# First layer in seven products for 15 blocks in place of 10, with sums kept in PSUM banks, in a chunked-attention and two-layer kernel

## The chip, the cores and the metric

The kernel runs on one core of a Trainium2 chip. The metric is the device time of one execution in microseconds (us). The core's engines work side by side, each through its own list of instructions in order: PE (TensorE, the matrix products), DVE (VectorE), ACT (ScalarE), POOL (GpSimd), and SP, which here only issues DMAs. PE reads from SBUF and writes into PSUM, which has eight banks of 512 f32 per partition. POOL also issues the DMAs that load and convert f32 to f16.

## What is computed

```python
# q, k, v: (8, 8, 576, 64) f32; batch, heads, sequence, head size
q_c, k_c, v_c = (a.reshape(B, H, 9, 64, D) for a in (q, k, v))     # chunks of 64
scores = np.matmul(q_c, k_c.transpose(0, 1, 2, 4, 3)) / np.sqrt(D)
scores = scores - scores.max(-1, keepdims=True)
attn = np.exp(scores); attn = attn / (attn.sum(-1, keepdims=True) + 1e-09)
x = np.matmul(attn, v_c) ... .reshape(4608, 512)                   # tokens x (heads * D)
h = x @ w_in                                                       # w_in: 512 x 2048
g = np.maximum(0.01 * h, h)
out = g @ w_out                                                    # w_out: 2048 x 512
```

There are 4608 tokens. Each chunk of 64 tokens attends only to itself.

## The kernel before, in words

**Units.** Attention goes in 36 units of 128 tokens (two chunks, all heads). For unit u: `g` loads q and k as f16 (POOL's queue; unit 0 as f32 on the queues of SP and ACT); `tq`, `tk` transpose q and k on PE (units 0 to 13), or `tdq`, `tdk` by DMA on SP's queue (from unit 14); `q`/`cq` copies q into a block-diagonal tile with zeros, `k` copies k; `s` gives the scores (8 matmuls of 64 columns); `m`, `b`, `x` are the maximum, the subtraction and the exponential; `z`, `n` the sum and the normalization (`n` on DVE for u < 10, then on POOL); `e` and `c` transpose the weights on PE and copy them, `d` does the same by DMA; `v` multiplies by v (8 matmuls of 64 columns); `a` copies the result, the tokens' x, into the ring `xT`.

**Blocks.** The two layers go in blocks: two of 128 tokens and 17 of 256 (`BLOCKS`).

*First layer.* Blocks 0 to 8 take it directly: `M` (`mm1`, L311), 16 groups of 128 hidden features by 4 matmuls each, per 128 or 256 tokens, into PSUM banks of 512 columns; `G` (`act1`, L328) applies the leaky function on ACT into `gT`. Blocks 9 to 18 take it in seven products instead of eight (a block of 256 tokens is halved in tokens, features and inner dimension, as in Strassen's and Winograd's scheme): `w_in_sum` (L351) forms four sums of the weights once, `x_sums` (L368) four sums of the block's x, and `wide` (L389; `V` j.s.n, product n of half s) makes each product with 8 matmuls of 128 columns. Products 1, 6, 7 and 4 accumulate one on the other in one bank, 2 and 5 have banks of their own, 3 adds to 5. After products 1, 6 and 7 ACT copies the bank into SBUF (`wide_x`, L442, `lx`); DVE adds the second, fifth and third product to these copies (`wide_m`, L449, `la`); ACT then applies the leaky function to the sums in SBUF (`leaky_kept`, `lp`), and to the bank itself after product 4. Per block and half: three copies, three adds, four leaky steps.

*Second layer.* Blocks 0 and 1 take it directly (`mm2`, L456, 512 columns a matmul; `store`). Blocks 2 to 18 take it in seven products: `weight_sum` (L169) once, `token_sums` (L182, `sum`) four sums of `gT` of 1024 f16 columns each (on DVE, but for eight on POOL), `product` (L205, `R` j.n) 8 matmuls of 256 columns each, `combine` (L251, `comb`): copies on ACT (n = 1, 6, 7, 4) and adds on DVE (n = 2, 5, 3, and 0 where a product has a bank to itself).

**Banks.** Four PSUM banks (m0 to m3) go round in a written order (`BANKS`, L154); the other four are fixed: `qp`, `kp` (transposes), `Sp` (scores) and `ox` (the transposed weights and the result of `v`), shared with some products.

**Order.** The string `ORDER` (L735) names every step; each engine executes its own part of it in that order. The loads up to unit 8 stand ahead of it in a string of their own (`LOADS`, L142): g1, the identity, then g2 g3 v0 Q0 Q1 g4 Q2 Q3 (v0: both halves of the first batch of v, Q: quarters of w_in, P: of w_out). `i` (`idle`, L682) are PE matmuls on a constant, counted in units of 128 columns: 111 in all, every one ahead of the first first-layer matmul. They keep PE running while the first units are on their way through the other engines.

```python
for what in ORDER.split():
    name = what.rstrip("0123456789.")
    how = [int(x) for x in what[len(name):].split(".") if x]
    STAGES[name](*how)
```

## Time and profile before

| | us |
|---|---|
| median of 3 runs | 275.94 (275.6 to 276.06) |
| span of the profiled execution | 273.3 |
| mean granted PE clock | 1.000 |

The profile is of one execution. Its span runs from the first to the last instruction; the device time is taken around it, so the two differ. A line of a group reads: source line, engine, operation, out<-in, shape, count | time busy in us, mean duration of one in ns | idle time of the engine just before them, and what ended it. In a timeline, rows begin with the start and the duration in us. DMA issues have the size of one and the median time to its landing.

### The profile page before, as it was taken

What the parts mean: (1) busy time and instruction counts of PE and PEld (TensorE: products, weight loads), DVE (VectorE), ACT (ScalarE), POOL (GpSimd) and SP (SyncE); (2) the same over time, 40 slices, a digit from 0 to 9 for tenths busy, and PEclk for the clock granted to TensorE, in tenths of its full rate; (3) what the DMA queues carried; (4) which work ended last, traced back from release to release, by engine and by line L of the source; (5) the groups of instructions that cost most, each with busy time, mean ns of one, the idle gap of its engine ahead of it and who ended that gap; (6) DMA issues with size and microseconds to landing.
All of it is one profiled execution on the core that took longest, in us unless ns stands there. A gap on an engine that the chain in (4) does not pass through costs nothing.

```text
span 273.3 us, 9009 instructions
## 1 busy us (share of the span) xinstructions
PE 265.9 (97%) x3705; PEld 242.4 (89%) x3705; DVE 219.9 (80%) x427; ACT 208.8 (76%) x410; POOL 165.3 (60%) x190
## 2 busy tenths in 40 slices
PE   7889999999999999999999999999999999999994
PEld 3579958999999899998989999999999998999994
DVE  7786869999997668798677987977899879488783
ACT  6667635665779688666999989899999998857560
POOL 8848546783175448649689799689895636012100
PEclk9999999999999999999999999999999999999999
DMA  9999999999999999999999999799999503131113
GB/s 147 155 188 191 206 178 156 176 117 130 210 138 169 171 140 119 195 219 168 164 189 153 203 160 124 139 134 180 95 147 158 134 2 101 22 98 40 41 41 115
DMA packets 159241, 38.34 MB, mean 140 GB/s; under 512 B 150240, under 2 KB 154720, under 8 KB 159200
## 3 DMA queue, kind: packets, MB, share of 16 engines
q0 software_dynamic: 111392, 18.10, 98.3%
q1 hardware_dynamic: 46768, 19.41, 38.7%
q8 instruction: 29, 0.48, 0.7%
q10 hardware_dynamic: 1040, 0.26, 0.4%
q14 instruction: 12, 0.10, 0.2%
HBM read 36.70 MB, written 9.44 MB: 169 GB/s over the span
## 4 chain that ended last, share of the span: by engine, by line
PE 86%; DVE 5%; ACT 3%; POOL 3%; issue 2%; POOLq 0%; DVEq 0%; ACTq 0%
PE hT L319 20%; PE prX L227 20%; PE xbank L416 11%; PE xpr L416 9%; PE prZ L227 6%; PE pr L227 6%; PE prW L227 3%; PE Sp L584 3%; PE xp L656 3%; PE oP L462 3%; ACT QZ L539 1%; ACT gT L435 1%; PE kp L512 1%; PE qp L512 1%; POOL SG L203 1%
## 5 line engine op out<-in xcount | busy, mean ns | idle before, releaser
L319 PE MATMUL hT<-xT,w_inT 128*128 128x128 f16 (+1 forms) x768 | 62.4, 237 | 0.0
L319 PEld LDWEIGHTS <-w_inT 128*128 128x128 f16 x768 | 53.6, 98 | 2.8
L227 PEld LDWEIGHTS <-SG 128*128 128x128 f16 x544 | 51.0, 98 | 5.4
L620 POOL TENSOR_TENSOR en<-ex,zi 128x512 f16<-128x512 f16 x26 | 28.2, 1085 | 40.1 <-DVE zi L614 19.8
L453 DVE TENSOR_TENSOR xkeep<-xpr,xkeep 128x512 f32<-128x512 f32 x60 | 39.6, 681 | 13.7 <-ACT xkeep L447 9.6
L333 ACT ACTIVATE gT<-hT 128x512 f16<-128x512 f32 x64 | 36.6, 595 | 9.0 <-PE hT L319 8.9
L227 PEld LDWEIGHTS <-gT 128*128 128x128 f16 x400 | 37.3, 98 | 4.3 <-ACT gT L435 0.4
L447 ACT ACTIVATE xkeep<-xbank 128x512 f32<-128x512 f32 x60 | 34.6, 593 | 7.4 <-PE xbank L416 7.0
L416 PEld LDWEIGHTS <-WS 128*128 128x128 f16 x640 | 38.0, 98 | 0.5
L91 POOL DMA_DIRECT2D q_in<-in_q_dram x39 | 33.4, 861 | 7.0 <-DMA w_outT<-in_moe_w_out_dram 3.0
L91 POOL DMA_DIRECT2D k_in<-in_k_dram x39 | 32.6, 838 | 7.8 <-DMA VB<-in_v_dram 3.3
L227 PE MATMUL prX<-TW,SG 128*128 128x256 f16 x272 | 35.3, 273 | 0.0
L435 ACT ACTIVATE gT<-xkeep 128x512 f16<-128x512 f32 x56 | 33.4, 631 | 2.1 <-DVE xkeep L453 1.8
L260 ACT ACTIVATE keep<-prX 128x256 f32<-128x256 f32 x51 | 19.6, 384 | 16.9 <-PE prX L227 16.5
L416 PEld LDWEIGHTS <-w_inT 128*128 128x128 f16 x480 | 29.0, 98 | 0.9 <-issue 0.4
L203 DVE TENSOR_TENSOR SG<-gT 128x1024 f16<-128x1024 f16 x34 | 25.2, 740 | 4.7 <-ACT gT L333 2.9
L610 DVE TENSOR_REDUCE z<-ex 128x8 f32<-128x512 f16 x36 | 24.4, 679 | 4.9 <-ACT ex L604 4.7
L593 DVE TENSOR_REDUCE mx<-Sp 128x8 f32<-128x512 f32 x36 | 24.4, 677 | 4.5 <-PE Sp L584 4.5
L573 ACT ACTIVATE QZ<-QT 64x512 f16<-64x512 f16 x44 | 27.3, 627 | 0.9 <-PE Sp L584 0.3
L677 ACT ACTIVATE xT<-xp 128x512 f16<-128x512 f32 x36 | 21.5, 596 | 6.0 <-PE xp L656 5.8
L387 POOL TENSOR_TENSOR xs<-xT 128x256 f16<-128x256 f16 x18 | 12.5, 701 | 20.7 <-ACT xT L677 20.7
L98 POOL DMA_DIRECT2D VB<-in_v_dram x24 | 23.4, 987 | 0.0
(92 smaller groups left out, 486.0 us busy)
## 6 DMA issues: line engine op xcount, KB each, us to landing
out_dram<-osb SPq DMA_DIRECT2D x35, 256.0 KB, 4.1
q_in<-in_q_dram POOLq DMA_DIRECT2D x31, 128.0 KB, 5.9
k_in<-in_k_dram POOLq DMA_DIRECT2D x31, 128.0 KB, 6.7
VB<-in_v_dram POOLq DMA_DIRECT2D x8, 288.0 KB, 9.1
VB<-in_v_dram POOLq DMA_DIRECT2D x16, 144.0 KB, 5.3
w_inT<-in_moe_w_in_dram POOLq DMA_DIRECT2D x8, 256.0 KB, 7.2
w_outT<-in_moe_w_out_dram POOLq DMA_DIRECT2D x4, 512.0 KB, 11.6
q_in<-in_q_dram POOLq DMA_DIRECT2D x8, 64.0 KB, 6.3
```

Of the source, the lines that this page charges most:

```text
L91: nc.gpsimd.dma_start(out=to, in_=rows)
L203: (nc.gpsimd if (j, n) in SG_POOL else nc.vector).tensor_tensor(out=SG[j, n], in0=x, in1=y, op=op)
L227: nc.tensor.matmul(out=to[:, i, :], lhsT=left[:, f, i * 128:(i + 1) * 128], rhs=right[:, f, :], start=(j, where) not in opened, stop=(f == ...
L319: nc.tensor.matmul(out=hT[:, i, :], lhsT=w_inT[:, t, fc * 128:(fc + 1) * 128], rhs=xT[:, t, r0:r0 + tb], start=(t == 0), stop=(t == NT - 1),)
L333: nc.scalar.activation(out=gT[j][:, nf * a:nf * a + nf, c0:c0 + tb], in_=HT.pop((j, a, p)), func=AFT.Prelu, bias=0.0, scale=1.0, alpha=0.01,)
L416: nc.tensor.matmul(out=to[:, i, :], lhsT=left[:, t, i * 128:(i + 1) * 128], rhs=right[:, t], start=(n in (1, 2, 5) and t == 0 and i == 0), ...
L435: nc.scalar.activation(out=gT[j][:, f0:f0 + 4, hi * 128:hi * 128 + 128], in_=of, func=AFT.Prelu, bias=0.0, scale=1.0, alpha=0.01)
L447: nc.scalar.activation(out=XK[j, s, n], in_=XB[j, s], func=AFT.Copy, bias=0.0, scale=1.0)
L453: nc.vector.tensor_tensor(out=to, in0=of, in1=to, op=ALU.add)
L573: nc.scalar.activation(out=to, in_=QT[u][part], func=AFT.Copy, bias=0.0, scale=1.0)
L593: nc.vector.tensor_reduce(out=MX[u], in_=SP[u], axis=AXL.X, op=ALU.max)
L620: (nc.gpsimd if u >= UP else nc.vector).tensor_tensor(out=E[u], in0=ex, in1=ZI.pop(u).unsqueeze(2).to_broadcast((128, 8, CH)), op=ALU.mult)
```

## The change

What it does:

- `BLOCKS` becomes 18 blocks of 256 tokens. Blocks 0 to 2 have the direct first layer, in parts of 128 tokens; blocks 3 to 17, 15 of them, have it in seven products. All 18 have the second layer in seven products, and nothing calls `mm2` any more.
- The sums of the first layer change. After product 1 its bank is copied into a second PSUM bank (`wide_seed`, `ls`), and product 2 accumulates there on top of the copy. After product 6, DVE adds the first bank to an SBUF copy of product 5 (`wide_five`, `lf`) and writes the sum back into the bank of product 5 (`wide_add`, `la` with n = 3), where product 3 accumulates on it. After product 7 DVE adds once more, into SBUF (`la` with n = 7). The leaky steps (`lp`) read PSUM in three cases of four. Per block and half: two copies, two adds, four leaky steps.
- All eight PSUM banks go round in one written order, for every use.
- `tq`, `tk` are on PE for units 0 to 10, by DMA from 11 on (50 DMA transposes in place of 44).
- A step with a `'` runs on its other engine: `sum`, `n`, `xs` on POOL in place of DVE, copies (`q`, `k`, `cq`, `c`, `a`, `ls`, `lf`, `comb`) and `lp` on DVE in place of ACT, `y` on ACT in place of DVE. In `ORDER` as it is now, POOL has 33 of 72 token sums (8 of 68 before), 32 of 60 x sums (36 of 40), 22 normalizations (26); DVE has 22 of the copies of `comb` (0 before), 25 of 50 `cq` (0 of 44), 12 of 60 `ls` and `lf`, 8 of 120 leaky steps (4).
- `ORDER` is written anew, with the loads in it. POOL begins with g1, the identity, L0.0 (half of the first v), Q3.0 (half a quarter of w_in), g2, g3, g4, L0.1, Q3.1, g5, Q1.0. The idle matmuls are 151 units. The sums of the weights are formed in halves, in the first part of the order. `z` is three steps.

The diff, cut to its core:

```diff
-    BLOCKS = 2 * [128] + 17 * [256]
-    EARLY = (2, 3, 4)
+    NB = 256
+    BLOCKS = 18 * [256]
+    LATE = (0, 1, 2)
+    FIVE = (0, 1, 2, 15, 16, 17)
+    HELD = 3
...
+    def ps(shape, name, kind=FP32):
...
+        return psp.tile(shape, kind, name=name, tag="m" + next(banks), bufs=1, padded_shape=padded)
...
     def wide(j, s, n):
...
-        if n in (1, 6, 7, 4):
-            if n == 1:
-                tag = "kp" if s else "Sp"
...
+        if n == 1:
+            XB[j, s] = ps([128, 4, 128], "xbank")
+        elif n == 5:
+            XZ[j, s] = ps([128, 4, 128], "xz")
+        to = {2: XW, 3: XZ, 5: XZ}.get(n, XB)[j, s]
         for i in range(4):
             for t in range(2):
                 nc.tensor.matmul(
                     out=to[:, i, :],
                     lhsT=left[:, t, i * 128:(i + 1) * 128],
                     rhs=right[:, t],
-                    start=(n in (1, 2, 5) and t == 0 and i == 0),
+                    start=(n in (1, 5) and t == 0 and i == 0),
...
-    def wide_x(j, s, n):
-        if n == 4:
-            leaky(j, s, 0, 1, XB.pop((j, s)))
-            return
-        XK[j, s, n] = sbp.tile([128, 4, 128], FP32, name="xkeep", tag="xkeep", bufs=6)
-        nc.scalar.activation(out=XK[j, s, n], in_=XB[j, s], func=AFT.Copy, bias=0.0, scale=1.0)
-
-    def wide_m(j, s, n):
-        of = XM[j, s, n]
-        to = XK[j, s, {2: 1, 5: 7, 3: 6}[n]]
-        nc.vector.tensor_tensor(out=to, in0=of, in1=to, op=ALU.add)
+    def wide_seed(j, s, other=0):
+        XW[j, s] = ps([128, 4, 128], "seed")
+        copy(other, XW[j, s], XB[j, s])
+
+    def wide_five(j, s, other=0):
+        X5[j, s] = sbp.tile([128, 4, 128], FP32, name="x5", tag="xkeep", bufs=6)
+        copy(other, X5[j, s], XZ[j, s])
+
+    def wide_add(j, s, n):
+        to = XZ[j, s] if n == 3 else X5[j, s]
+        nc.vector.tensor_tensor(out=to, in0=XB[j, s], in1=X5[j, s], op=ALU.add)
+
+    def wide_leaky(j, s, n, other=0):
+        second, hi = {2: (0, 0), 4: (0, 1), 3: (1, 0), 5: (1, 1)}[n]
+        of = {2: XW, 4: XB, 3: XZ, 5: X5}[n][j, s]
+        f0 = 8 * s + 4 * second
+        leaky(other, hidden(j)[:, f0:f0 + 4, hi * 128:hi * 128 + 128], of)
...
     ORDER = (
...
+        "g1 y0' y1' I y3 y4' If i38.0 tq0 L0.0 q0.1 y2 q0.0' tk0 k0 i4.1 tq1 s0 m0 tk1 Q3.0 q1.1 k1' q1.0' b0 i21.2 s1 m1 "
+        "b1 x0 x1 z0.0 g2 i33.3 tq2 q2.1 i5.4 tk2 k2 g3 i5.5 tq3 q3.0 z1.0 g4 q3.1 z0.1 z0.2 L0.1 q2.0' n0 z1.1 s2 m2 "
+        "i2.6 e0 z1.2 b2 Q3.1 i12.7 tq4 c0 x2 tk3 n1 i6.8 e1 k3' i22.9 v0 s3 z2.0 q4.1 c1 v1 g5 z2.1 z2.2 tk4 a0 n2 e2 "
+        "Q1.0 M0.3.1 a1 m3 b3 c2 x3 v2 a2 k4' M0.3.2 q4.0' z3.0 z3.1 s4 tq5 tk5 k5 z3.2 M1.3.1 q5.0' n3 i3.10 e3 q5.1 s5 "
...
+        "cq11.0 z10.1 V3.0.2 lf3.0 g14 R1.4 V3.0.6 lp3.0.2 V3.1.1 ls3.1 la3.0.3 cq12.0 s11 m11 comb1.4' sum1.4 R2.6 b11 "
+        "V3.1.6 la3.1.3 V3.0.7 xs3.4' comb2.6 x11 g15 R2.7 V4.1.1 V3.1.2 sum2.4 la3.0.7 z11.0 z10.2 tdq14 v9 a9 xs4.1' "
```

More of the change, by code (lines that the diff above doesn't have):

```diff
@@ L497, with idle, copy @@
+    def idle(n, _=0):
+        t = ps([128, 512], "idle")
+        for i in range(0, n, 3):
+            c = 128 * min(3, n - i)
+            nc.tensor.matmul(out=t[:, :c], lhsT=warm[:, :128], rhs=warm[:, :c], start=True, stop=True)
+    def copy(other, to, of):
+        if other:
+            nc.vector.tensor_copy(out=to, in_=of)
+        else:
+            nc.scalar.activation(out=to, in_=of, func=AFT.Copy, bias=0.0, scale=1.0)
     QP: dict[int, bass.AP] = {}
@@ new lines, in last_product @@
+    def last_product(left, right):
+        r0 = START[LAST] + halves_of(LAST)[1].start
+        for c in range(0, HM, HM // 2):
+            cut = slice(c, c + HM // 2)
+            of = ps([128, HM // 2], "prL")
+            for f in range(HF):
+                nc.tensor.matmul(out=of, lhsT=left[:, f, :], rhs=right[:, f, cut], start=(f == 0), stop=(f == HF - 1))
+            to = ob[LAST, 1][:, cut]
+            nc.vector.tensor_tensor(out=to, in0=of, in1=kept[LAST, 7][:, cut], op=ALU.add)
+            nc.sync.dma_start(out=out[r0:r0 + 128, cut], in_=to)
```

765 lines of the change are left out of this document (296 added, 469 removed), and 170 rows, old and new, of the table ORDER.

## The prediction, made before the changed kernel ran

> **What bounds the kernel now.** I read the page's head first, then TensorE's (PE's) rows in order of time.
>
> ```profile
> span 273.3 us, 9009 instructions
> PE 265.9 (97%) x3705; PEld 242.4 (89%) x3705; DVE 219.9 (80%) x427; ACT 208.8 (76%) x410; POOL 165.3 (60%) x190
> ...
> PE   7889999999999999999999999999999999999994
> ...
> PEclk9999999999999999999999999999999999999999
> ...
> GB/s 147 155 188 191 206 178 156 176 117 130 210 138 169 171 140 119 195 219 168 164 189 153 203 160 124 139 134 180 95 147 158 134 2 101 22 98 40 41 41 115
> ```
>
> PE is busy 97% of the span, at full granted clock, and short of nine tenths only in the first three slices of 6.8 us and the last. A busy PE may still be slowly fed, so the next view is the timeline of PE alone; there the distance between the starts of two neighbouring rows, divided by the count of the first, is the true pace.
>
> ```profile
> 181.04 0.40 PE L656 MATMUL xp<-et,VB 128*128 128x64 f16 x8
> 181.28 1.06 PE L416 MATMUL xbank<-xT,WS 128*128 128x128 f16 x16
> 182.17 1.04 PE L227 MATMUL prX<-TW,gT 128*128 128x256 f16 x8
> 183.04 1.06 PE L416 MATMUL xpr<-xs,w_inT 128*128 128x128 f16 x16
> ...
> 29.68 3.74 PE L319 MATMUL hT<-xT,w_inT 128*128 128x128 f16 x64
> 33.26 0.39 PE L512 MATMUL kp<-ident,k_in 128*128 128x128 f16 x4
> ...
> 34.37 1.89 PE L462 MATMUL oP<-w_outT,gT 128*128 128x512 f16 x8
> 36.10 0.40 PE L584 MATMUL Sp<-KT,QZ 128*128 128x64 f16 x8
> ...
> L416 PEld LDWEIGHTS <-WS 128*128 128x128 f16 x640 | 38.0, 98 | 0.5
> ```
>
> 16 matmuls of 128 columns take 182.17 - 181.28 = 0.89 us, 55.6 ns each; 64 of them in the plain first layer 3.58 us, 55.9 ns; 256 columns 0.87 / 8 = 109 ns; 512 columns 1.73 / 8 = 216 ns; 64 columns 0.24 / 8 = 30 ns. Time follows the number of columns with almost nothing on top, and the weight loads (last row, a lines view: 98 ns each) hide behind the matmuls before them. **PE's columns set the time**; there are no waits in the middle worth winning.
>
> **The change, part by part.** *Columns.* Five more blocks of 256 tokens have a first layer in seven products. They add 5 x 112 = 560 matmuls of 128 columns, and remove the direct form of 1280 tokens: 128 matmuls of 128 columns and 256 of 256. 31.1 - (7.2 + 27.9) = **-4.0 us**. The first 256 tokens go through the second layer in seven products: 56 matmuls of 256 columns for 32 of 512: 6.1 - 6.9 = **-0.8 us**. Units 11 to 13 are transposed by DMA: 24 PE transposes of 128 columns less, **-1.3 us**. Together -6.1 us, call it -6.0 for the 176 more instructions that each have their own small cost.
>
> Here a rule of the Trainium skill speaks against the change. "TensorE: Matmul & The Clock Gate", section "Back-to-back issue gap", gives about 81 ns as the sustained spacing of 128-column matmuls in a real kernel and 131 ns at 512, since weight loads count; on a line between them 256 columns cost 98 ns, and the first-layer term would be 45.4 - (10.4 + 25.1) = +9.9 us. This trace disagrees (55.6 and 109 ns); the same page's isolated formula, N/2.4 + 2.5 ns, fits it.
>
> *The start.* Two things move there: the idle matmuls that keep PE running grow from 111 units of 128 columns to 151, all but three of them ahead of the first first-layer matmul, and POOL issues its loads in another order.
>
> ```profile
> 1.33 3.50 PE L686 MATMUL idle<-warm 128*128 128x384 f16 x11 [1.33 <-DVE zeros L137]
> ...
> 7.43 0.41 PE L584 MATMUL Sp<-KT,QZ 128*128 128x64 f16 x8 [0.72 <-DVE QZ L541]
> ...
> 11.59 2.07 PE L686 MATMUL idle<-warm 128*128 128x384 f16 x13
> 14.01 0.40 PE L628 MATMUL tpe<-ident,en 128*128 128x128 f16 x4 [0.35 <-DVE en L620]
> ...
> 15.09 0.39 PE L656 MATMUL xp<-et,VB 128*128 128x64 f16 x8
> ...
> 17.44 1.95 PE L319 MATMUL hT<-xT,w_inT 128*128 128x128 f16 x32
> ...
> 15.02 0.68 POOL L91 DMA_DIRECT2D k_in<-in_k_dram  x1 [2.17 <-DMA VB<-in_v_dram]
> ...
> q_in<-in_q_dram POOLq DMA_DIRECT2D x31, 128.0 KB, 5.9
> ...
> VB<-in_v_dram POOLq DMA_DIRECT2D x8, 288.0 KB, 9.1
> ...
> w_inT<-in_moe_w_in_dram POOLq DMA_DIRECT2D x8, 256.0 KB, 7.2
> ```
>
> An idle unit costs 2.07 us / 39 = 0.053 us, at the cold start 3.50 / 33 = 0.106. Ahead of the first first-layer matmul (17.44 now) come 37 more, five of them cold: 2.2 us; and tq4, tk4, s3 and e2 (0.9 us), which is work done early and not lost. If the present waits stayed, the loss would be 2.2 us; if the added idle work only fills waits, nothing; if it took the two longest waits shown, 0.72 and 0.35, with it, -1.1. Then the loads: VB was needed at 15.09 and had landed by 15.02, after 6 x 128 + 2 x 288 = 1344 KB of POOL's queue. Now Q3.0 (256 KB) and g4 (256 KB) stand ahead of its second half: 1856 KB. In strict order and at the same pace it lands at 15.0 x 1856 / 1344 = 20.7; by the GB/s row (6.8 us a slice; 1.0 + 1.1 MB by 13.7 us, less 0.5 MB of the two f32 loads on other queues, then 188 KB a us) that many bytes have moved by 15.4. I take 17.5, near their middle; the first layer follows some 1.2 us later (v0, a0), at 18.7: 1.3 later, less 0.9 of work done early. **Value +0.8 us, ends -1.1 and +3.6** (20.7 + 1.2 - 17.4 - 0.9).
>
> *Work of the other engines.*
>
> ```profile
> sum 273.30, PE 265.88 PEld 242.36 DVE 219.92 ACT 208.84 POOL 165.27; mean PE 18.99 PEld 17.31 DVE 15.71 ACT 14.92 POOL 11.80
> ...
> L453 DVE TENSOR_TENSOR xkeep<-xpr,xkeep 128x512 f32<-128x512 f32 x60 | 39.6, 681 | 13.7 <-ACT xkeep L447 9.6 <-PE xpr L416 3.9
> L203 DVE TENSOR_TENSOR SG<-gT 128x1024 f16<-128x1024 f16 x34 | 25.2, 740 | 4.7 <-ACT gT L333 2.9 <-ACT gT L435 1.8
> L203 DVE TENSOR_TENSOR SG<-SG,gT 128x1024 f16<-128x1024 f16 x17 | 11.9, 699 | 0.8
> L203 DVE TENSOR_TENSOR SG<-gT,SG 128x1024 f16<-128x1024 f16 x9 | 7.2, 795 | 0.1
> L281 DVE TENSOR_TENSOR osb<-prZ,keep 128x256 f32<-128x256 f32 x22 | 9.3, 421 | 4.6 <-PE prZ L227 3.1 <-ACT keep L260 1.2
> L541 DVE COPY QZ<-qp 64x512 f16<-64x512 f16 x19 | 7.9, 417 | 1.8 <-ACT QZ L539 1.5 <-PE qp L512 0.2
> L387 DVE TENSOR_TENSOR xs<-xT 128x256 f16<-128x256 f16 x2 | 0.6, 282 | 0.0
> L447 ACT ACTIVATE xkeep<-xbank 128x512 f32<-128x512 f32 x60 | 34.6, 593 | 7.4 <-PE xbank L416 7.0 <-DMA out_dram<-osb 0.2
> L333 ACT ACTIVATE gT<-hT 128x512 f16<-128x512 f32 x64 | 36.6, 595 | 9.0 <-PE hT L319 8.9
> L203 POOL TENSOR_TENSOR SG<-gT,SG 128x1024 f16<-128x1024 f16 x8 | 17.4, 2173 | 9.3 <-DVE SG L203 4.0 <-ACT keep L260 2.7 <-ACT xkeep L447 2.6
> L620 POOL TENSOR_TENSOR en<-ex,zi 128x512 f16<-128x512 f16 x26 | 28.2, 1085 | 40.1 <-DVE zi L614 19.8 <-ACT xkeep L447 9.8 <-ACT gT L435 3.0
> ```
>
> A block in seven products now needs per half two copies and two adds besides its four leaky steps, not three and three; so the adds of L453 stay 60 for 15 blocks. ACT loses 60 copies of L447 and 40 steps of L333 (58.4 us) and gains 48 copies into PSUM or SBUF and 36 leaky steps, at some 0.6 us 50 us; DVE takes over half of the QZ copies. ACT only gets lighter. A copy from PSUM into PSUM isn't shown; L447 (593) is the nearest row, and ten per cent of it on 24 copies would not matter to an engine at 76%. DVE: 21 token sums go (-15.5); 16 copies of 512 columns come at the 681 of L453 (+10.9), 22 of 256 columns at 421 (+9.3), 25 QZ copies at 417 (+10.4), 24 x sums at 282 (+6.8), four normalizations and four leaky steps more at about 0.7 (+5.6), the rest about -5: **+22, from 220 to 242 us, 90% of a span of 269**. POOL: 25 more token sums at 2173 (+54), four normalizations less (-4): 165 to 215 us, 80%. No engine passes PE, but DVE's cover gets thin.
>
> *The waits added.* Before, the sixth, seventh and fourth products of a half waited for ACT's copies of their bank; now the second and sixth wait for the copy into the seeded bank, and the third, seventh and fourth for DVE's adds (la). All of PE is queued behind a late add, the products of the second layer too. In the new order V6 and V7 of a half stand some 2.0 us of PE apart (V3.0.6 to V3.0.7: 8 + 8 matmuls of 128 columns, 8 of 64, 8 of 256 = 2.0), the add takes 0.68: about 1.2 us of slack. What can eat it is this:
>
> ```profile
> L203 DVE TENSOR_TENSOR SG<-gT x34: 640/684/1979, 30.3 to 265.7; 128x1024 f16<-128x1024 f16 x34
> ...
> 204.40 1.98 DVE L203 TENSOR_TENSOR SG<-gT 128x1024 f16<-128x1024 f16 x1
> 204.76 1.06 POOL L620 TENSOR_TENSOR en<-ex,zi 128x512 f16<-128x512 f16 x1
> ```
>
> A DVE sum, median 684 ns, took 1979 where it met a POOL operation on SBUF (its row begins earlier, but ends 0.56 us after POOL's). The Trainium skill has this as a rule: "SBUF — State Buffer", section "Who interferes with whom": a DVE instruction with two SBUF inputs and a GpSimd instruction that reads SBUF exclude each other, and the second waits for the first's end. The trace agrees; the adds of L453, with one input in PSUM, are no victims themselves, but queue behind one.
>
> By mean less median the sums lost 34 x 56 ns = 1.9 us in all. POOL's two-input work grows from 71 to 118 us and DVE's steps that can meet it, by count, from 75 to 126: 2.8 times, some +4 us of DVE time, of which a part reaches PE. **Value +1.2 us, ends 0 and +8** (each of the 25 new POOL sums holding PE up for a quarter of the 1.3 us lengthening above).
>
> Nothing else counts: six more DMA transposes go on SP's queue, where an end is awaited several steps later; loads keep their number; the tail (last product, add, store) is the same.
>
> **Sum:** -6.0 + 0.8 + 1.2 = -4.0, a span of 269.3. The median of 275.94 lies 2.6 above the profiled span, so 271.9: I say **272.0**.
>
> **Rivals.** (1) *The lock of DVE and POOL decides: slower.* If a POOL sum makes one DVE step ahead of an add 1.3 us longer, 33 x 1.3 = 43 us; DVE's busy time passes the span's 269 from 21 of the 33 on. At 24 it is 242 + 31 = 273, with some 4 us that DVE stands still at start and tail now as then: 277 + 2.6 = **280**. For: DVE at 90%, 80% of POOL. Against: nine tenths of the sums now run at their median. 0.16. (2) *The start eats the gain:* loads in strict order, first v step 20.7 instead of 15.09, 5.6 late, less 0.9: -6.0 + 4.7 + 1.2 = -0.1, **275.8**. For: POOL waited 2.17 us for VB. 0.10. (3) *Seven products don't pay:* if in the new order no 128-column matmul went faster than its weight load, 98 ns, the first-layer term would be 54.9 - (12.5 + 27.9) = +14.5, 18.5 above the one taken: **290.5**; the 55.6 ns of this kernel speak against it. 0.03. (The rule of "TensorE: Matmul & The Clock Gate" above, in the Trainium skill, points this way.) (4) *The waits go too:* the start loses its waits and DVE stalls nowhere, -7.1: **268.8**. 0.07.
>
> **Numbers.** Forecast 0.64, rivals as above. A difference of 0.2% (0.55 us) is about what a measurement can tell. Faster: 0.64 + 0.07 = 0.71 and a little of rival 2: 0.72. Same 0.09, slower 0.19. The range, 268.8 to 278.0, holds the forecast with its ends, rivals 2 and 4 and the near part of rival 1.
>
> **What would show it.** 1680 matmuls of L416's kind at 55 to 56 ns, PE's column time 6 us less; the first first-layer matmul near 18.7; DVE near 242 and POOL near 215 busy; DVE sums with medians near 690 and few above 1000; PE at nine tenths in all slices but the first three and the last. Wrong would be: PE idle in the middle released by DVE adds (rival 1), or a first-layer start past 21 us (rival 2).

## The result, and the profile after

| | before | after |
|---|---|---|
| median | 276.00 us (275.6 to 276.79) | 309.29 us (305.44 to 310.64, 4 runs) |
| ratio to before | 1 | 1.1127, 95% interval 1.1059 to 1.1194 |
| span of the profiled execution | 273.3 us | 306.7 us |
| mean granted PE clock | 1.000 | 0.972 |

The changed kernel is 33 us slower by these medians, and 31 by the ratio. The ratio leaves out slow runs, those over 1.5% above a kernel's fastest: of the changed kernel it takes 305.44 and 308.50, with the middle at 306.97. The forecast was 272.0, four faster. The page of the changed kernel (spans and busy times, rows of 40 slices, the chain that ended last):

```profile
span 306.7 us, 9459 instructions
...
PE 273.2 (89%) x3893; PEld 248.3 (81%) x3893; DVE 261.5 (85%) x494; ACT 184.4 (60%) x355; POOL 218.4 (71%) x207
...
PE   7799987888996989979989979889839999989995
...
DVE  3769999999995998899899999788997986787664
...
PEclk9969999979999999999999999999978999999999
...
PE 46%; DVE 33%; DMA 12%; issue 5%; POOL 2%; ACT 1%; DVEq 0%; POOLq 0%; ACTq 0%
```

Before, PE was busy 97% of the span, and the chain read so:

```profile
PE 86%; DVE 5%; ACT 3%; POOL 3%; issue 2%; POOLq 0%; DVEq 0%; ACTq 0%
```

Now PE is at 89% of the span and 46% of the chain, and the share that is missing belongs to DVE and to DMAs. PE's row has 7s and 8s from one end to the other and one 3; the lost time is not in one stage. Two sums follow from the head. PE's columns fell, and yet PE is busy 7 us longer than before (273.2 against 265.9): where it stood idle, the granted clock dropped behind the gap (the 6, 7 and 8 in the PEclk row). The remainder is idle time: 306.7 - 273.2 = 33.5 us against 273.3 - 265.9 = 7.4.

The view of waits (engine and line, what it waited for: us in total, times, longest) names many small ones; these are PE's:

```profile
PE prX L513 <- DVE ob L551: 6.3, 2, 5.8
...
PE qp L217 <- DMA q_in<-in_q_dram: 2.4, 2, 1.5
PE prX L513 <- DVE TW L472: 2.4, 1, 2.4
PE xp L323 <- DMA et<-en: 2.4, 4, 1.2
PE xbank L430 <- DVE x L449: 2.4, 3, 0.9
```

PE waits for DVE's last adds (`ob`), its weight sums (`TW`) and its first-layer adds (`x`), and for loads and DMA transposes. No single wait explains 33 us. The largest of them, in the timeline (start and duration in us; DVE, then POOL, then PE):

```profile
218.30 0.68 DVE L449 TENSOR_TENSOR x<-xbank,x 128x512 f32<-128x512 f32 x1
218.90 6.34 DVE L406 TENSOR_TENSOR xs<-xT 128x256 f16<-128x256 f16 x1
225.16 1.26 DVE L289 TENSOR_REDUCE z<-ex 128x8 f32<-128x512 f16 x2
...
218.35 0.67 POOL L406 TENSOR_TENSOR xs<-xT 128x256 f16<-128x256 f16 x1
218.98 1.04 POOL L297 TENSOR_TENSOR en<-ex,z 128x512 f16<-128x512 f16 x1
219.97 0.90 POOL L112 DMA_DIRECT2D VB<-in_v_dram  x1
220.88 2.13 POOL L490 TENSOR_TENSOR SG<-gT,SG 128x1024 f16<-128x1024 f16 x1
222.96 2.11 POOL L490 TENSOR_TENSOR SG<-gT 128x1024 f16<-128x1024 f16 x1
...
219.26 1.04 PE L513 MATMUL prX<-TW,SG 128*128 128x256 f16 x8
...
227.23 1.86 PE L513 MATMUL prX<-w_outT,gT 128*128 128x256 f16 x8 [5.81 <-DVE ob L551]
```

A DVE step with two SBUF inputs (`xs`), 282 ns in the median of its group, takes 6.34 us. It ends at 225.24, a moment after the last of an unbroken train of POOL steps (222.96 + 2.11 = 225.07). The `ob` that PE needs is queued behind it on DVE. PE stands still for 5.81 us, and its next eight matmuls take 1.86 us where eight of the same size took 1.04 before the gap: the clock has dropped too, to a granted 0.50 between 227.2 and 232 us.

The start came late. In PE's timeline the first product with v and the first first-layer matmuls:

```profile
22.38 0.40 PE L323 MATMUL xp<-et,VB 128*128 128x64 f16 x8
...
23.52 1.06 PE L358 MATMUL hT<-xT,w_inT 128*128 128x128 f16 x16
```

These stood at 15.09 and 17.44 before. And PE's pace where it isn't disturbed, later in the same timeline:

```profile
240.15 1.06 PE L430 MATMUL xbank<-xT,w_inT 128*128 128x128 f16 x16
241.04 1.04 PE L513 MATMUL prX<-TW,SG 128*128 128x256 f16 x8
241.91 0.40 PE L323 MATMUL xp<-et,VB 128*128 128x64 f16 x8
```

0.89 us for 16 matmuls of 128 columns and 0.87 for 8 of 256: 55.6 and 109 ns, as before the change.

### The profile page after: what moved, and what is told of

It is laid out like the page before. It is cut to its first block, busy times and chain, and to the rows that moved or that the text cites. A ratio compares the mean times of both kernels' runs of the same rounds, so it can differ in the third digit from the quotient of the medians.

```text
span 306.7 us, 9459 instructions
## 1 busy us (share of the span) xinstructions
PE 273.2 (89%) x3893; PEld 248.3 (81%) x3893; DVE 261.5 (85%) x494; ACT 184.4 (60%) x355; POOL 218.4 (71%) x207
## 3 DMA queue, kind: packets, MB, share of 16 engines
q0 software_dynamic: 111392, 18.10, 85.6%
## 4 chain that ended last, share of the span: by engine, by line
PE 46%; DVE 33%; DMA 12%; issue 5%; POOL 2%; ACT 1%; DVEq 0%; POOLq 0%; ACTq 0%
PE prX L513 13%; PE xbank L430 9%; PE prZ L513 5%; PE xz L430 5%; DVE SG L490 4%; DMA et<-en 3%; DVE xs L406 3%; DMA q_in<-in_q_dram 3%; PE prW L513 3%; DVE z L291 3%; DVE mx L274 3%; DVE z L289 3%; DMA KT<-k_in 3%; PE seed L430 2%; DVE x L449 2%
## 5 line engine op out<-in xcount | busy, mean ns | idle before, releaser
L430 PEld LDWEIGHTS <-WS 128*128 128x128 f16 x960 | 59.4, 99 | 7.0 <-issue 6.1
L430 PEld LDWEIGHTS <-w_inT 128*128 128x128 f16 x720 | 44.2, 98 | 4.0 <-issue 3.2
L490 POOL TENSOR_TENSOR SG<-gT 128x1024 f16<-128x1024 f16 x16 | 35.7, 2230 | 12.8 <-PE prZ L513 5.7
L297 POOL TENSOR_TENSOR en<-ex,z 128x512 f16<-128x512 f16 x22 | 27.1, 1235 | 22.1 <-DVE z L293 17.0
L430 PE MATMUL xbank<-xs,WS 128*128 128x128 f16 x480 | 35.3, 219 | 2.2 <-DVE xz L449 2.2
L372 ACT ACTIVATE gT<-xbank 128x512 f16<-128x512 f32 x30 | 17.7, 595 | 15.2 <-PE xbank L430 11.5
L513 PE MATMUL prX<-w_outT,gT 128*128 128x256 f16 x144 | 19.3, 280 | 7.3 <-DVE ob L551 6.3
L358 PE MATMUL hT<-xT,w_inT 128*128 128x128 f16 x384 | 24.3, 219 | 1.8 <-DVE sh L278 1.8
L490 POOL TENSOR_TENSOR SG<-gT,SG 128x1024 f16<-128x1024 f16 x10 | 21.9, 2191 | 4.7 <-DVE SG L490 3.9
L449 DVE TENSOR_TENSOR xz<-xbank,x 128x512 f32<-128x512 f32 x30 | 20.3, 690 | 4.5 <-PE xbank L430 2.8
```

What stands on the lines that cost most here:

```text
L297: (nc.gpsimd if other else nc.vector).tensor_tensor(out=EN[u], in0=EX[u], in1=Z[u, 2].unsqueeze(2).to_broadcast((128, 8, CH)), op=ALU.mult)
L358: nc.tensor.matmul(out=hT[:, i, :], lhsT=w_inT[:, t, fc * 128:(fc + 1) * 128], rhs=xT[:, t, r0:r0 + tb], start=(i == 0 and t == 0), stop=( ...
L372: nc.scalar.activation(out=to, in_=of, func=AFT.Prelu, bias=0.0, scale=1.0, alpha=0.01)
L430: nc.tensor.matmul(out=to[:, i, :], lhsT=left[:, t, i * 128:(i + 1) * 128], rhs=right[:, t], start=(n in (1, 5) and t == 0 and i == 0), st ...
L449: nc.vector.tensor_tensor(out=to, in0=XB[j, s], in1=X5[j, s], op=ALU.add)
L490: (nc.gpsimd if other else nc.vector).tensor_tensor(out=SG[j, n], in0=x, in1=y, op=op)
```

## The experiments

Theory: the lock between DVE's two-input steps and POOL's reads (rival 1 of the prediction). Rivals: DVE's plain load, POOL's lateness, the new first layer's waits, the start, the DMA path. All times are medians in us; "before" was 275.1 to 275.5 beside these runs. Steps of a few us are read with the spread of the runs: a kernel with waits varies more than the one before (275.6 to 276.79). In the order strings a `'` behind a step puts it on its other engine.

### POOL's steps: off, or without their reads

All 87 elementwise steps of POOL go to DVE:

```diff
-  ... comb1.1' ... sum0.4' ... n11' ... xs4.1' ...
+  ... comb1.1' ... sum0.4  ... n11  ... xs4.1  ...
```

> The changed kernel with all 87 elementwise operations of POOL (33 token sums, 32 x sums, 22 normalizations) on DVE; POOL only issues DMAs. Theory (lock: DVE steps with two SBUF inputs stand still while POOL reads SBUF): no DVE step over 1.3 times its median is left; DVE gains about 33 x 0.69 + 22 x 0.69 + 32 x 0.28 = 47 us of work and loses the 40 us or so by which its steps are lengthened, so it is busy about 265 us and the time stays near 300, 292 to 308, now bound by DVE's plain load. Rival (load: DVE is simply too full, the lock matters little): 47 us more on the engine that bounds, 330 or more. Rival (start and loads decide): 309 as it was.

Measured 316.94 (ratio 1.1504, interval 1.1470 to 1.1538), with DVE 262.3 busy and POOL 96.3. Between the two expectations. Taking the lock away by giving DVE the work brings nothing: what DVE no longer loses to the lock it spends on the steps themselves, and they stand ahead of what PE needs.

The small steps that the lock hits, taken out (the addition of 1e-9 to the sums; 25 copies of q from DVE to ACT):

```diff
-  nc.vector.reciprocal(out=Z[u, 2], in_=Z[u, 1])
+  nc.vector.reciprocal(out=Z[u, 2], in_=Z[u, 0])
-  ... cq14.0' ...
+  ... cq14.0 ...
```

> The changed kernel without the 36 small adds of 1e-9 to the sums of the exponentials (the sums are at least 1, so the result is the same in f32), and with the 25 f16 copies of QT into QZ that DVE has put on ACT. Some 20 of the 42 lengthened DVE steps are of these two kinds, about 17 us of lengthening, and their own plain work is 36 x 0.09 + 25 x 0.25 = 9 us. Theory (lock): DVE's busy time falls by 20 to 26 us, to about 238, and the time by 10 to 25 us, to 285 to 299. Rival (load alone): DVE falls by 9 us and the time by at most 9, to 300 or more. Rival (start and loads): 309, no change.

Measured 305.0 (1.1087; 303.23 to 307.71), 4 us less than the changed kernel's median, with runs that overlap, where 10 or more were expected: a miss. The small victims cost DVE time (248.6 us busy in place of 261.5), but little of it reached PE.

POOL's steps in their places, of about the same length, but hardly reading SBUF:

```diff
-  (nc.gpsimd if other else nc.vector).tensor_tensor(out=SG[j, n], in0=x, in1=y, op=op)
+  nc.gpsimd.memset(SG[j, n], 0.01)      # twice
+  nc.gpsimd.tensor_tensor(out=SG[j, n][:, 0:HF:4, 0:4], in0=..., in1=..., op=op)
```

and so for `xs` and `n`.

> The changed kernel with each elementwise operation of POOL replaced by two memsets of its output and one small tensor_tensor on a few columns of the same inputs, so that POOL stands as busy at the same places and waits for the same steps but hardly reads SBUF. The token sums, x sums and normalizations of POOL are left out by it. Theory (lock on reads): the DVE sums run at their median again, only the QZ copies may still be held; DVE's busy time falls by 25 to 40 us and the time to 270 to 285. Rival (load alone, or POOL too late with its sums): DVE's plain work and POOL's are as before, so 300 to 309.

Measured **291.81** (1.0597, interval 1.0552 to 1.0642), above the expected range, but 17.5 us below the changed kernel's median (15.2 below the middle of the runs that the ratio takes); its highest time, 293.1, is 12 us below the changed kernel's lowest. The groups of DVE's two-input steps, and one kind with a single SBUF input (`QZ<-QT`) (line, out<-in, shapes, count | busy, mean ns of one | idle before), in the changed kernel:

```profile
L490 DVE TENSOR_TENSOR SG<-gT 128x1024 f16<-128x1024 f16 x20 | 17.8, 896 | 2.8 <-POOL SG L490 2.0 <-PE prZ L513 0.4 <-ACT gT L372 0.3
...
L291 DVE TENSOR_TENSOR z<-z,tiny 128x8 f32<-128x8 f32 x36 | 14.1, 397 | 0.4
...
L188 DVE COPY QZ<-QT 64x512 f16<-64x512 f16 x25 | 12.5, 499 | 1.2 <-DMA QT<-q_in 0.8
L406 DVE TENSOR_TENSOR xs<-xT 128x256 f16<-128x256 f16 x15 | 11.9, 792 | 0.0
...
L370 DVE SCALAR_TENSOR_TENSOR gT<-x 128x512 f16<-128x512 f32 x8 | 9.0, 1121 | 0.0
```

and with POOL only writing:

```profile
L504 DVE TENSOR_TENSOR SG<-gT 128x1024 f16<-128x1024 f16 x20 | 13.5, 680 | 4.1 <-POOL SG L183 2.8 <-PE prZ L527 0.8 <-ACT gT L380 0.5
L193 DVE COPY QZ<-QT 64x512 f16<-64x512 f16 x25 | 12.9, 517 | 3.5 <-DMA QT<-q_in 3.1
...
L296 DVE TENSOR_TENSOR z<-z,tiny 128x8 f32<-128x8 f32 x36 | 5.5, 159 | 0.4
...
L378 DVE SCALAR_TENSOR_TENSOR gT<-x 128x512 f16<-128x512 f32 x8 | 5.5, 683 | 0.0
...
L417 DVE TENSOR_TENSOR xs<-xT 128x256 f16<-128x256 f16 x15 | 4.3, 284 | 1.3 <-ACT xT L195 1.1
```

The same steps on the same shapes, 896 against 680 ns, 397 against 159, 792 against 284, 1121 against 683. The longest of each kind fell from 2015, 1971, 6336 and 2635 ns to 693, 168, 293 and 691. By the pages DVE's busy time falls from 261.5 to 229.9: POOL's reads lengthened DVE's work by 31.6 us. Of the maxima (DVE's reduction) and the adds with one input in PSUM nothing changed (679 and 682, 690 and 692 ns). This is what the Trainium skill says in "SBUF — State Buffer", section "Who interferes with whom": a DVE step with two SBUF inputs contends with a GpSimd instruction that reads SBUF, not with one that only writes it. The trace agrees on who is hit. It does not bear out that the second waits for one instruction: the 6.34 us above outlasted four POOL operations and a DMA issue between them. DVE's 25 copies of q from SBUF to SBUF (`QZ<-QT`) have one such input and are held all the same, also by a POOL that only writes: 499 and 517 ns on average, against 319 in the first run above, where POOL has no elementwise step.

One more thing changes with the edit: the memsets don't wait for POOL's inputs, so POOL's steps can end sooner after them. In the changed kernel's waits PE never waits for a POOL step, and DVE for one sum only, 2.0 us, so little of the gain can come from there directly.

The lock away in another manner: none of POOL's elementwise steps, no small additions, and DVE's copies and leaky steps on ACT, so that DVE has 230 and ACT 217 us.

```diff
-  ... n11' ... lp3.1.5' ... comb3.1' ... cq14.0' ...
+  ... n11  ... lp3.1.5  ... comb3.1  ... cq14.0  ...
```

> The changed kernel with POOL's 87 elementwise operations on DVE, without the 36 small adds, and with the QZ copies, the copies of combine, of the seeds, of the fifth product and of x, and the last leaky steps that DVE has put on ACT (ACT is busy 184 us of 307). DVE's plain work: 261 - 40 (lengthening) + 47 - 36 x 0.09 - 25 x 0.25 - 22 x 0.34 - 16 x 0.6 - 8 x 0.6 = about 235 us; ACT about 220. Theory (lock): nothing is held, PE's work is 6 us less than before the change, so 270 to 282. Rival (load): DVE at 85 per cent of the span in an order made for other durations stalls PE anyway, 285 to 300. Rival (start and loads): 305 or more.

Measured 313.27 (1.1383): a miss by 30 us. Without any lock, and with evenly loaded engines, it is as slow as with it; PE's longest waits there are for DMA transposes of the weights (9.5 us in five places). Every step at another place or of another length can be late for someone; moved work isn't a clean test of the lock, and the write-only kernel is a cleaner one.

### What is not the rest

About half of the loss is found, 15 to 17.5 us. The next runs ask what the other 16 are, most of them starting from the write-only kernel.

Loads of q and k two places earlier in POOL's queue, everything else as changed:

```diff
-  ... g14 ... g15 ...
+  ... g16 ... g17 ...
```

> The changed kernel with the q and k loads of units 11 to 35 two places earlier in POOL's list of loads, nothing else moved. Now a load is issued 12 to 27 us ahead of its unit's scores (25 to 45 in the kernel before), and stands in POOL's queue behind operations that wait for data. Theory (the part of the loss that the lock doesn't explain comes from loads and DMA transposes that land too late): the leads grow by some 10 us, waits of PE for transposed tiles and QZ copies fall from about 8 us to 3 or less, and the time by 4 to 10 us, to 299 to 305. Rival (the order is short of lead everywhere, in copies and adds above all): at most 2 us better, 307 or more.

311.93 (1.1307): no gain. The write-only kernel without the small additions and with the copies of q on ACT (the two edits above together):

> The run whose POOL only writes (token sums, x sums and normalizations of POOL left out), and on top without the 36 small adds of 1e-9 and with the 25 QZ copies of DVE on ACT, so that no kind of DVE step that was held up is left beside a busy POOL. Theory (the lock is over with the POOL reads; what remains, 16 us above the kernel before, is of another kind): no better than 3 us below that run's 291.8, so 288 to 293, though DVE has 18 us less to do. Rival (the held QZ copies and small adds were still part of it): 280 to 287.

294.64 (1.0698), no better than 291.81: what was left of the lock, the held copies of q, cost no time. The same without any sum and reciprocal of the weights (all `z` left out):

> The same, and all of z left out (the 36 sums of the exponentials and the 36 reciprocals too; the normalization multiplies by a constant): another 30 us less for DVE, which is then busy about 180 us, less than in the kernel before. Theory (DVE's plain load in an order with little slack makes the rest of the loss): the time falls to 272 to 281. Rival (the order's chains of ACT, DMA, POOL and PE are too close whatever DVE does): at most 5 us below the run without this, 284 or more.

296.82 (1.0736) with DVE at 190 us busy: **DVE's load is not the rest**. The write-only kernel with one memset instead of two, POOL at 169 us:

> The run whose POOL only writes, with one memset in place of two: POOL's steps take half as long (token sums about 1.2 us in place of 2.2), POOL's busy time falls by some 54 us. Same parts left out. Theory (POOL is late with its sums and with the loads queued behind them): 8 to 16 us below that run's 291.8, so 276 to 284. Rival (POOL's lateness isn't the rest): 288 or more.

292.06 (287.55 to 294.08, where 276 to 284 would have been POOL's lateness): **POOL's length is not the rest** either.

### Parts of the change alone, in the order of before

33 of 68 token sums on POOL:

```diff
-  SG_POOL = ((8, 4), (9, 4), ..., (15, 4))
+  SG_POOL = ((5, 4), ..., (17, 4), (5, 3), ..., (17, 3), (10, 2), ..., (16, 2))
```

> The kernel before, with nothing changed but that 33 of its 68 token sums stand on POOL, as many as in the changed kernel (8 before): n = 4 and n = 3 of blocks 5 to 17 and n = 2 of blocks 10 to 16. Theory (lock): 25 more sums of 2.17 us on POOL hold DVE steps with two SBUF inputs, as they did in the changed kernel, where a POOL that hardly reads SBUF was 17 us faster; DVE's plain work falls by 18 us, but ten or more of its steps take over 1.3 us and the time goes up by 8 to 25 us, to 284 to 300. Rival (the old order has slack for it, the new one lacks it): 275 to 279.

299.42 (1.0867, interval 1.0818 to 1.0916), as expected. The same with those sums write-only:

> The same 33 token sums of the kernel before on POOL, but each as two memsets of its output and one small tensor_tensor on a few columns of its inputs (those 33 sums are left out): POOL as busy, with the same waits, hardly reading SBUF. Theory (lock): at least half of what the run with real sums on POOL lost comes back. Rival (POOL is just late with its sums, 2.17 us each in place of 0.69, and PE waits for them): the same time as with the real sums, within 3 us.

290.86 (1.0559). 8.6 of the 24 us come back, somewhat over a third and not the expected half. Most of the remainder is that a POOL sum takes three times as long as a DVE sum (medians of 2128 and 684 ns in the kernel before), and here PE waits for it. From the waits of the first of the two:

```profile
PE prX L227 <- POOL SG L203: 11.2, 10, 2.4
```

In the second it still waits 9.3 us for them, in nine places.

The new first-layer sums alone, for the ten blocks that had seven products, the steps around them moved no more than their data demand:

```diff
-  lx9.0.1 ... V9.0.2 ... la9.0.2 ... V9.0.6 ... lx9.0.6
+  ls9.0   ...            V9.0.6 V9.0.2     ... lf9.0 la9.0.3 ... V9.0.7 la9.0.7
```

> The kernel before with only the sums of the first layer made as in the change, for its ten blocks: after product 1 its bank is copied into a second PSUM bank and product 2 accumulates there, product 5 is copied to SBUF, and the adds after products 6 and 7 are DVE's, into PSUM and SBUF; the two leaky steps that read PSUM come right behind products 2 and 3. Where the seeded bank was last used by a product of 256 columns, half of the seed is overwritten. Per block two copies and two adds less. Theory (the order and the lock are what costs, not the form of the sums): within 6 us of the kernel before, 272 to 282, the upper half because PE now waits for an add where it waited for a copy, in an order not made for it. Rival (the form costs: PE behind DVE's adds): 290 or more.

323.01 (1.1728): in the rival's range. DVE and ACT have less to do than before (209 and 202 us busy), and PE waits, longest for the adds:

```profile
PE xbank L418 <- DVE xpr L467: 13.4, 11, 3.0
```

The form with fewer copies puts an add of DVE between products 6 and 7, and 7 and 4, which share a bank, where a copy of ACT stood. In this order, which gives the add no lead, it costs far more than it saves. The adds aren't all of it: of some 44 us that PE stands idle, 13.4 are for these adds, 6.5 for leaky steps and 4.5 for seed copies.

Four more DMA transposes (q and k of units 12 and 13) for 16 PE transposes:

```diff
-  tq12 Q12 tk12 k12 ... tq13 Q13 tk13 k13
+  tdq12 cq12.0.1 cq12.1.1 tdk12 ... tdq13 cq13.0.1 cq13.1.1 tdk13
```

> The kernel before with q and k of units 12 and 13 transposed by DMA and copied by ACT in place of PE's transposes, nothing else. Theory (PE's columns set the time of the old order): 16 transposes of 128 columns less, 16 x 55.6 ns = 0.9 us faster, 274.2 against 275.1. Rival (the DMA transposes land too late, or ACT's 627 ns copies in place of DVE's hold PE up): no change or slower by up to 2 us.

282.49 (1.0253, interval 1.0222 to 1.0285): 7.4 us slower where 0.9 faster was expected. Most of it is one wait of PE, in its timeline:

```profile
83.66 0.58 PE L656 MATMUL xp<-et,VB 128*128 128x64 f16 x8 [4.63 <-DMA et<-en]
```

The transposed weights `et` come from SP's queue. Its timeline in this kernel:

```profile
77.30 1.19 SPq L558 DMA_TRANSPOSE KT<-k_in  x1
78.59 1.20 SPq L643 DMA_TRANSPOSE et<-en  x1
```

the step of PE just ahead of the first row, from the chain:

```profile
77.03 0.23 PE Sp L584 x8
```

and the same two transposes in the kernel before:

```profile
70.05 1.23 SPq L558 DMA_TRANSPOSE KT<-k_in  x1
71.39 1.21 SPq L643 DMA_TRANSPOSE et<-en  x1
```

With one more k in flight by DMA, the transpose of k for unit 15 finds, by the order of the steps, the ring of three `KT` buffers full, and is issued right after the scores that end at 77.26; the weights of unit 9 stand behind it on SP's queue, 7.2 us later than before, and PE's product behind them. PE's granted clock was 0.83 between 70 and 90 us. The wait is one of order on SP's queue; that the DMA engines were full isn't shown to be its cause. This run turned the search to the DMA path. The page of before had shown it to be full:

```profile
DMA  9999999999999999999999999799999503131113
```

The 16 DMA engines are at nine tenths in 30 of the first 31 slices, some 205 us.

### The DMA path and the sums' waits, with the lock away

From here on the short write-only kernel (292.06) is the base. First, everything that a DMA transpose writes is replaced, for its reader, by one constant tile; all DMAs are still issued:

```diff
-  copy(other, QZ[...], QT[u][part])
+  copy(other, QZ[...], fixed_k[part])
-  qz, kt = QZ[u % NQZ], KT[u]
+  qz, kt = QZ[u % NQZ], fixed_k if u in QT else KT[u]
```

and so for `et` in `v`.

> The kernel with short write-only POOL work (292.06) in which, besides, the scores, the copies of q and the products with v read one constant tile for every unit whose operands came by a DMA transpose. All DMA transposes and loads are still issued, but nothing on PE, ACT or DVE waits for them from unit 11 on. Theory A (the rest of the loss, 292 against 276, is the chain load, DMA transpose, copy, scores): 276 to 282. Rival B (the rest is the chain of copies and adds between the products of the new first layer): 288 to 292. Rival C (short waits of every kind, each replaced by the next): 283 to 288.

288.74 (283.15 to 290.38). The ranges of the two kernels overlap, so a gain isn't shown; theory A's 276 to 282 is out. The same edit on the changed kernel, lock and all:

> The changed kernel (309.29) with the same constant tile in place of what the DMA transposes write, all of POOL's work as it was. If the lock and the DMA chain add up: 309 less what the DMA waits are worth in the kernel without the lock, so 295 to 300 under theory A. Rival (with the lock the DMA chain is hidden behind DVE's lengthened steps): 305 to 309.

308.85 (1.1165), unchanged: under the lock no gain is seen either. The base without the seed copy and DVE's two adds of a half:

```diff
-  start=(n in (1, 5) and t == 0 and i == 0),
+  start=(n in (1, 2, 5) and t == 0 and i == 0),
-  copy(other, XW[j, s], XB[j, s])
-  ... la3.0.3 ... la3.0.7 ...
```

The copy of product 5 (`lf`) stays.

> The kernel with short write-only POOL work (292.06) in which the seed copy into the second bank and DVE's two adds of a half are left out, so that no product of the first layer waits for a copy or an add of its own half (product 2 starts a bank of its own, product 3 accumulates on product 5). DVE has 60 adds less, ACT and DVE together 30 copies less. Rival B (the new first layer's waits are the rest): 276 to 282. Theory A (DMA chain): 288 to 292. Rival C (every kind, each replaced by the next): 284 to 289.

291.42 (286.94 to 293.02): no gain shown by itself, and rival B's 276 to 282 is out. Both:

> Both at once: no seed copies and adds, and the constant tile for what the DMA transposes write; POOL short and write-only. All theories: the sum of the two gains if they are independent, so 272 to 278, near the 270 of the forecast's columns; above 282 would mean that a third kind of wait (leaky steps, second-layer copies, the start) is as large.

285.22 (1.0346, interval 1.0309 to 1.0383; 283.8 to 286.18). That is 6.8 us below the base's median, but only 1.4 lie between its highest time and the base's lowest (287.55), and the constant tile alone came down to 283.15. So the two are worth between 1 and 7 us together, and whether each had hidden the other isn't shown. It is far above the 272 to 278 that was expected. In its chain of waits, and in its list of them:

```profile
124.06 8.53 DMA out_dram<-ob
...
132.69 0.43 DVE ob L568
...
133.16 1.00 PE prX L530 x5
...
DVE ob L568 <- DMA out_dram<-ob: 11.2, 5, 4.4
```

A store of 256 KB, whose median landing takes 3.3 us, lands after 8.53; until then its buffer isn't free, DVE's next add into that ring waits (4.4 us), and PE behind it. The next kernel drops the DMA transposes themselves, which nothing reads there any more:

```diff
-  nc.sync.dma_start_transpose(...)      # in tdk, tdq and d
```

> The kernel with neither wait (285.22) without the DMA transposes themselves: what they write is read by nothing there, and SP's queue then holds the output stores alone. Loads, engines' work and PE's columns stay. In the trace of the kernel with neither wait DVE's last adds (ob) wait 11.2 us in 5 places for stores that stand behind DMA transposes on SP's queue, and PE waits 8 us behind them between 120 and 135 and near 184. Theory D (stores behind transposes on SP's queue are the third part): 276 to 279, and no wait of DVE for a store left. Rival E (DVE's adds were late for another reason, or the start is the whole rest): 283 to 285.

**274.43** (0.9958, interval 0.9938 to 0.9977; 273.38 to 275.11): 10.8 us less, more than the 6 to 9 expected, and no wait of DVE for a store is left. A store's median landing is 2.4 us. Its page (rows of the queues: packets, MB, the time of their packets as a share of 16 engines' span):

```profile
span 273.0 us, 9185 instructions
...
PE 263.8 (97%) x3893; PEld 244.4 (90%) x3893; DVE 188.2 (69%) x428; ACT 171.7 (63%) x331; POOL 169.7 (62%) x295
...
PE   8788999999999999999999999999999999999995
...
PEclk9999999999999999999999999999999999999999
...
q0 software_dynamic: 111392, 18.10, 88.4%
q1 hardware_dynamic: 6512, 9.70, 10.0%
```

PE is at 97% and full clock again. Against the same two rows with the transposes:

```profile
q0 software_dynamic: 111392, 18.10, 97.2%
q1 hardware_dynamic: 50032, 20.20, 40.9%
```

80 transposes were 43520 packets, 544 each. Without them the packet time of the same 111392 packets of the loads is 88.4% of 273.0 us, or 241 us, where it was 97.2% of 284.4, or 276 (the shares of two queues can add up to more than 100%, so packets overlap). In the other kernels with transposes it is 260 to 295 us, in the one below 249: the loads' packets were slower beside the transposes. The Trainium skill has a rule that fits in "DMA: Bandwidth & Descriptors", section "Issuing engines are not separate DMA queues": DMAs issued from different engines end up on the same 16 DMA engines and interleave there. The trace is in line with it, by the 241 against 276 us. What this run doesn't separate is how much of the 10.8 us is that contention and how much is that stores no longer stand behind transposes on SP's queue.

Last, the start: POOL's first loads in an order close to that of before.

```diff
-  g1 I L0.0 Q3.0 g2 g3 g4 L0.1 Q3.1 g5 Q1.0
+  g1 I g2 g3 L0.0 L0.1 Q3.0 g4 Q3.1 g5 Q1.0
```

> The kernel before it in this list, with POOL's first loads in another order: g2, g3, both halves of the first v, Q3.0, g4, Q3.1, g5, Q1.0, as near to the order of the kernel before the change as the new order of the first layer allows. In the changed kernel the first product with v starts at 22.38 us instead of 15.09 and the first first-layer matmul at 23.52 instead of 17.44. Theory F (the loads' order makes the start late, rival 2 of the prediction): the first first-layer matmul near 18.5 to 20, and 3 to 5 us less than the kernel without transposes. Rival G (the start is late for the 151 idle units and the f32 transposes, whatever the loads): the same time within 1 us.

273.18 (0.9909, interval 0.9876 to 0.9943; its runs, 271.19 to 275.44, straddle those of the kernel before it): 1.2 us by the medians, not 3 to 5, and not shown by runs that overlap. The wait moved to the next load; unit 4's q is now what PE waits for:

```profile
17.78 0.38 PE L220 MATMUL qp<-ident,q_in 128*128 128x128 f16 x4 [1.67 <-DMA q_in<-in_q_dram]
```

and the first first-layer matmul came at 21.36 instead of 21.81.

### The account

| kernel | median | lowest to highest | step of the median |
|---|---|---|---|
| changed | 309.3 | 305.4 to 310.6 | |
| POOL's reads away | 291.8 | 290.3 to 293.1 | -17.5 (-15.2 by the runs of the ratio) |
| POOL half as long | 292.1 | 287.6 to 294.1 | 0 |
| and nothing waits for a DMA transpose | 288.7 | 283.2 to 290.4 | -3 (ranges overlap) |
| and no seed copies or adds between the first layer's products | 285.2 | 283.8 to 286.2 | -3.5 (ranges overlap) |
| and no DMA transposes | 274.4 | 273.4 to 275.1 | -10.8 |
| and the first loads in another order | 273.2 | 271.2 to 275.4 | -1 (ranges overlap) |

Two steps are clear of the spread: POOL's reads, and the DMA transposes once nothing waits for what they write. The parts depend on their order: the fourth line alone shows no gain under the lock, and the fifth none alone. The transposes weren't taken away with the lock still there. The last kernels do less than the whole computation, so none of them is a version that beats the kernel before, and none was found.

## Why the prediction was wrong, step by step

- **Columns, -6.0: right.** The paces are 55.6 and 109 ns, unchanged. The 81 and 131 ns that the Trainium skill gives in "TensorE: Matmul & The Clock Gate", section "Back-to-back issue gap", by which the first layer would have got dearer, are not seen here either. Rival 3 is out. With the waits out of the way the kernel runs at 273.2 to 274.4, within 2.4 us of the forecast, at PE 97%; from the first first-layer matmul to the end of the span it takes 250.0 to 251.2 us, against 255.9 in the kernel before. That it comes so near is in part luck, since those kernels leave out work and start late. A mean clock of 0.972 hid it: the changed kernel's PE is busy 273.2 us for the same 3893 instructions that take 263.8 at full clock, so 9.4 us of the loss is slower matmuls, behind gaps like the one shown. The prediction had no term for that; it priced a wait at its length alone.
- **The start, +0.8, first first-layer matmul at 18.7: wrong.** It came at 23.52, beyond even the strict-order bound (20.7 for the first v step; it came at 22.38). Loads of q and k for units 2 and 3, which I had not timed, were late first: PE waited 1.50 us for one of them at 13.28. Behind these waits the granted clock was 0.56 between 16 and 22 us, for which the 18.7 had no term either. Rival 2's late loads came, but that their order was the cause isn't shown: with everything else away an order near that of before brought 0.5 us at that matmul and about 1 in all, so the idle matmuls and the loads themselves remain as causes.
- **DVE's load, 242: too high.** Without POOL's reads it is 229.9 us. POOL's 218.4 is as forecast (215), and ACT got lighter, as said (184.4). No engine passes PE, as said.
- **The lock, inside the term of +1.2 (ends 0 and +8): the mechanism was right, the size failed.** I took what 34 sums had lost in the kernel before (mean less median, 1.9 us) and scaled it by counts to some 4 us of DVE time. It was 31.6, and 15 to 17.5 us of the end. The term's own upper end, 8, was half of that, and the range stopped at 278.0, though the terms' upper ends add up to 281.5. Two things were missing. The hit steps are not only the sums, whose median (681 ns) stayed as forecast, but also the other steps with two SBUF inputs, down to 8 columns, and the copies of q. And POOL's work can come in a train: one step was held for 6.34 us, several POOL operations. No other held step took over 2.64, near the length of one POOL sum (2.13) and its own. Rival 1 had this mechanism at 0.16 and 280; it also expected DVE to become the bound, which it didn't (85% busy): PE waits in order behind single lengthened steps.
- **"About 1.2 us of slack" between products 6 and 7: wrong in kind.** It counted the add's own time and not what stands ahead of the add on DVE. In the changed kernel PE waits for these adds in six places, 6.1 us in all. The kernel with the new sums in the old order lost 48 us with emptier engines, though not by the adds alone. Here, with the lock away, taking the sums' waits out shows no gain as long as the DMA waits stay.
- **"Nothing else counts: six more DMA transposes go on SP's queue": wrong, and the step I priced at nothing.** Four of them cost 7.4 us in the order of before, through a full ring of buffers and what stood behind it on SP's queue; taking away all 80 brought 10.8 in the new one, with the lock away (74 of the 80 were there before the change, so this isn't the price of the six). The cover I named, "an end is awaited several steps later", was read from PE's order alone, not from SP's queue, nor from the DMA row of the page, full in 30 of the first 31 slices.
- **Signs named beforehand:** PE idle in the middle behind DVE's adds, and a first-layer start past 21 us. Both came.

Open: how the 10.8 us divide between the DMA engines and SP's queue; what the lock costs apart from the order it was met in; what the transposes cost under the lock; why the start was late; and whether another order of this same form would be faster than the kernel before, since no new order as a whole was tried.

## What to carry to other kernels

A sum of columns says what the bound engine could reach; where that engine is already at 97%, the change is decided by what its helpers share, so work moved to POOL is priced by the DVE steps with two SBUF inputs beside it, and a transpose moved to DMA by the buffers it needs and by what stands behind it on its queue, never at nothing; a full DMA row is a reason to look. A wait of PE costs its length and can cost the slower clock behind it (0.50 after 5.81 us here). To size such a cost, keep every step in its place and take the one shared thing away (reads, transposes): moving the work instead makes other steps late and hides the answer.

## What was not expected of the hardware

- A DVE step of 282 ns was held for 6.34 us, through four POOL operations and a DMA issue on POOL, without getting in between them. A copy from SBUF to SBUF, with one input, is held as well, by a POOL that only writes too (517 against 319 ns).
- An addition of 8 columns in f32 takes 397 ns on average beside POOL's reads and 159 without them, though it moves almost no data.
- 80 DMA transposes of 128 x 512 f16 make 43520 packets, and the packet time of the loads is 13% less when they are gone (241 against 276 us).
- Behind an idle 5.81 us eight matmuls of 256 columns took 1.86 us in place of 1.04, at a granted clock of 0.50.
